# Gated SyncE loads and pairwise first score blocks in a windowed attention plus MLP kernel

## Chip, core, metric

One core of a Trainium2 chip. The metric is the device time of one execution in microseconds; five executions of the kernel before took 262.74 to 263.31 us, median 263.27.

## What is computed

Attention with a window and sinks over 4 batches, 8 heads, 768 positions, head size 64, and then a token mixer and a two-layer MLP on its output (width 512, hidden 2048). Cut to its core:

```python
# attention: q, k, v are (4, 8, 768, 64)
scores = matmul(q, k.T) / sqrt(64)
keep = (key < 4) | (0 <= query - key < 128)          # 4 sinks, window 128
a = softmax(where(keep, scores, -1e9))
x = (a @ v) as (4, 768, 512)
# mixer
a1 = alpha1 * x + beta1
u = x + lam * einsum('ts,bsd->btd', w_tok, a1)       # w_tok 768 x 768
a2 = alpha2 * u + beta2
out = u + lam * (relu(a2 @ w_ch1) @ w_ch2)           # 512 -> 2048 -> 512
```

Inputs and output are float32; the kernel's matmuls are float16.

## The kernel before

The kernel works in tiles of 128 positions: six row tiles per batch (r, j or ti), heads in four pairs (hp) and two groups of four heads (G).

The steps for a batch, with their lines:

- **Loads.** q and k of a head pair (`load_qk`, L481) come through SyncE's queue in float32, 384 KB each; six of batch 0 come through GpSimd's queue, which casts to float16 on the way (L486). v comes by row tiles (L503; batch 0 by halves, `load_v0`, L520), w_tok by row tiles of 384 KB (L531), w_ch2 in blocks of 512 KB (`load_w`, L540), w_ch1 in four quarters of its hidden columns through GpSimd's queue (`load_w1`, L544; 512 KB written each, twice that read), lam at L1156.
- **Transposes** of q and k on TensorE (L594, L597), copied out to `qkT` by ScalarE or VectorE (L349, L351); from batch 2 on by DMA (L613).
- **Scores.** Per key tile j, a block S (L702), in the first batch for one group of four heads. S has two buffers in PSUM. In the first batch most blocks first get a mask added by a matmul of the identity with a bias (L697); the others are multiplied by a mask on VectorE afterwards (L731). ScalarE takes the exponential (L722). The sinks have their own product and exponential (L639, L644).
- **pv** (L785, L792), and on VectorE the division by the sum (L817, L818) to x; then `xh` = x * lam * alpha1 on GpSimd (L827, L834), and the beta term on VectorE (L841).
- **tok** (L916): six matmuls per row tile with the transposed w_tok; VectorE adds it to x (L923), ScalarE or GpSimd cast to u.
- **uTp** (L957): transposes of u, and alpha2, beta2 applied on ScalarE and VectorE (L940, L942).
- **h** (L996): 16 blocks of 128 hidden columns for each half batch, relu on ScalarE or VectorE (L1002, L1004). A quarter of w_ch1 serves four blocks.
- **ch** (L1052, L1023): the second product. w_ch2 is first multiplied by lam on VectorE or GpSimd (L898), from the buffers that L540 filled.
- **Out**: VectorE adds (L1063, L1032) and SyncE stores (L1066, L1035).

Batches overlap: the attention of the next batch is worked in among the MLP of this one.

The order of the work isn't written out. Each step is added to a `Plan` as a task with a priority, an engine or a choice of them with a cost in ns, the tasks that it needs, and the buffers that it uses. `Plan.run` goes through modelled time and gives each engine the ready task that can start first, ties by priority; the result is the order in which each engine's instructions stand in the program, and the engines keep to it. The model has two DMA rings (`Rings`): SyncE's and GpSimd's, which share the engines by turns. When the model says that a transfer has landed, its task is seen as done 300 ns later (L203). Where the model sees TensorE idle before 36 us, filler matmuls on zeros are put in (`idle`, L342). `emit` shuffles the priorities with the seeds in `TURNS` (L406) before it runs the plan, so that each list of seeds gives another order. `W1_SINCE` (L407) lets no request for w_ch1 be planned before 20 us.

`scores_by_pair` (L739) scores a key tile of the first batch, first group, pair by pair: two blocks of half the size, each with its own exponential, and one mask product. It is used for j < `PAIRS`, and `PAIRS` is 0 (L404), so it isn't used. The choice is made here (L1121):

```python
            if G == 0 and j < PAIRS:
                scores_by_pair(base + 10 * j, j, BIAS[0][j])
            else:
                scores(base + 10 * j, 0, j, (G,), bias=BIAS[G][j])
```

The requests of SyncE's queue for the second batch stand at L1152 to L1162: q and k, lam, w_ch2, v. Nothing but buffers, the model's times and priorities orders them against w_ch1.

Of the kernel before, what the change touches and what calls it, by code (L numbers as in the profile page):

```python
# [10 lines left out]
FP16 = mybir.dt.float16  # L11
# [4 lines left out]
PE, ACT, DVE, POOL, SP = "pe", "act", "dve", "pool", "sp"  # L16
# [13 lines left out]


FW = 1.0


class Rings:
# [74 lines left out]
class Plan:  # L110
# [9 lines left out]
    def add(self, prio, engs, fn, after=(), uses=(), mode=None, lands=None, port=False,  # L120
            since=0.0):


        t = Task(len(self.tasks), prio, engs, fn, after, uses, mode, lands, port, since)
        for a in t.needs:
            a.then.append(t)
        self.tasks.append(t)
        return t

    def run(self, prio):  # L130
# [17 lines left out]
        rings = Rings()  # L148
# [3 lines left out]
        def end(t, seen):  # L152
            t.seen = seen
            for b in t.uses:
                b.left -= 1
                b.freed = max(b.freed, seen)
                if b.left == 0:
                    busy[b.kind][b.home] = False
                    homes[b.kind][b.home] = b.freed
            for o in t.then:  # L160
                ready[o.i] = max(ready[o.i], seen)
                waiting[o.i] -= 1
                if not waiting[o.i]:
                    bisect.insort(open_, (rank[o.i], o.i))
# [33 lines left out]
        while len(steps) < len(tasks):  # L198
            best = pick()
            if best is None or landing <= best[0]:  # L200
                assert landing < float("inf"), "no task can go on"
                t = rings.step(float("inf"))
                end(t, rings.now + 300.0)  # L203
                landing = rings.peek()
                continue
            start, r, _, i, e = best
            open_.pop(bisect.bisect_left(open_, (r, i)))
            t = tasks[i]
            for b in t.uses:
                if b.home is None:  # L210
                    b.home = min((h, n) for n, (h, x) in enumerate(zip(homes[b.kind], busy[b.kind]))
                                 if not x)[1]
                    busy[b.kind][b.home] = True
            idle = None
            n = int((start - max(free[PE], 400.0)) / (took if free[PE] > 4500.0 else 110.0))
            if e == PE and free[PE] < until and n > 0:
                spare = [(h, k) for k, (h, x) in enumerate(zip(homes["d"], busy["d"])) if not x]
                if spare and min(spare)[0] <= free[PE]:
                    idle = (min(spare)[1], n)
                    homes["d"][idle[0]] = start  # L220
                    mode = None
            cost = t.engs[e]
            if t.lands:
                cost += rings.room("sw" if e == POOL else "hw", t.lands, start) - start
            if e == PE:
                if start < 4500.0:
                    cost = cost * 2
                if t.mode != mode:
                    cost = cost + 95
                mode = t.mode  # L230
            free[e] = start + cost
            if e == POOL or (e == DVE and t.port):
                port = free[e]
            steps.append((t, e, start, free[e], idle))
            if t.lands:
                rings.step(start)
                rings.issue("sw" if e == POOL else "hw", t, free[e])
                landing = rings.peek()
            else:
                end(t, free[e] + SEEN[e])  # L240
# [34 lines left out]
def kernel(  # L275
# [123 lines left out]
    w1f = const.tile([P, NC, DFF], FP16, name="w1f")  # L399
    w2f = const.tile([P, NF, DM], FP16, name="w2f")  # L400

    ROWS = 7000.0

    PAIRS = 0  # L404

    TURNS = (39286, 39315, 39323, 39754, 40467, 41250, 41382, 139002, 39003, 39015, 139040, 139062, 139089, 139154, 39159, 139160, 39171, 39387, 139559, 139625, 139757, 139905, 39966, 140019, 140036, 140073)  # L406
    W1_SINCE = 20000.0  # L407

    V0 = (((0, 1), (2, 3), (4, 5)), ((0, 1, 2), (3, 4, 5)))
# [90 lines left out]
    def load_v(p, b, r, wait=None):  # L500
        bf = vn[b, r] = Buf("vnat", None, None, f"vnat{b}_{r}")
        done["vn", b, r] = add(
            p, {SP: 550}, lambda e: nc.sync.dma_start(  # L503
                bf.t, v[b, :, r * P : (r + 1) * P, :].rearrange("h p d -> p h d")),
            [wait], [bf], lands=(64, 19.0))
# [31 lines left out]
    def load_w(p, key, src):  # L537
        bf = wst[key] = Buf("wst", None, None, f"wst_{key}")
        done["wst", key] = add(
            p, {SP: 400}, lambda e: nc.sync.dma_start(bf.t, src), uses=[bf], lands=(16, 90))  # L540

    def load_w1(p, i):
        done["w1", i] = add(
            p, {POOL: 760}, lambda e: nc.gpsimd.dma_start(  # L544
                w1f[:, :, i * 512 : (i + 1) * 512],
                moe_w_ch1[:, i * 512 : (i + 1) * 512].rearrange("(c p) f -> p c f", p=P)),
            lands=(32, 96), since=W1_SINCE)

    def load_w2(p, i):
        for a in range(4 * i, 4 * i + 4, 2):  # L550
# [541 lines left out]
    load_w1(-770, 0)  # L1092
    for i in range(1, 4):
        load_w1(-769, i)

    def fold_rows():
        for name, key, o, p in (("a1", "la1", la1_b, -987), ("b1", "lb1b", lb1_b, -986)):
# [36 lines left out]
    for b in range(B):  # L1134
        w0 = STEP * b
        if b == 0:
            seq = [("tok", ti) for ti in range(3)] + [("uT", 0, 0), ("uT", 0, 1)]
            seq += [("tok", ti) for ti in range(3, NR)]
            m1 = []
            for qd in range(4):  # L1140
                for chk in range(2):
                    m1 += [("m1", chk, fi) for fi in range(4 * qd, 4 * qd + 4)]
            m1.insert(3, ("uT", 1, 0))
            m1.insert(5, ("uT", 1, 1))
        else:
            seq = [("tok", ti) for ti in range(NR)]
            m1 = [("m1", 0, fi) for fi in range(NF)]
            m1 += [("m1", 1, fi) for fi in range(NF)]
        seq += m1
        seq += [("m2", ti, part) for ti in range(NR) for part in range(4)]  # L1150
        ns = len(seq)
        if b == 0:  # L1152
            for i, (hp, t) in enumerate(QK_ORDER):
                load_qk(t0 + 100 + i, 1, hp, t)
            done["lam"] = add(
                t0 + 150, {SP: 500}, lambda e: nc.sync.dma_start(  # L1156
                    lam_b, moe_lam.unsqueeze(0).to_broadcast([P, DM])), lands=(8, 90))
            for i in range(4):
                load_w2(t0 + 200 + i, i)
                cast_w2(w0 + 22 + 4 * i, i)  # L1160
            for r in range(NR):
                load_v(t0 + 300 + r, 1, r)  # L1162
        for i, (what, *args) in enumerate(seq):

            p = w0 + i - (LEAD if b and what == "tok" and args[0] < 3 else 0)
            {"tok": tok, "uT": uTp, "m1": mlp1, "m2": mlp2}[what](p, b, *args)
            if b and what == "tok":
                uTx(p + 0.3, b, *args)
        if b + 1 < B:
            nb = b + 1  # L1170
            if nb >= XB:
                for i, (hp, t) in enumerate(QK_ORDER):
                    load_qk(w0 + i, nb, hp, t, done["qkT", b, 3, 1])
                for r in range(NR):
                    load_v(w0 + 10 + r, nb, r, done["qkT", b, 3, 1])
            lo, hi = (1, ns - 14) if b else (LO, ns - 12)
            steps = [("T", i) for i in range(8)] + [("sk",)]
            for j in range(NR):
                steps += [("S", j)]
                steps += [("pv", j - 1, 0), ("pv", j - 1, 1)] if j else [("vs",)]  # L1180
            steps += [("pv", NR - 1, 0), ("pv", NR - 1, 1)]
            for r in range(NR):
                cast_v(w0 + lo + (hi - lo) * (r + 4) / len(steps), nb, r)
            for i, (what, *args) in enumerate(steps):
                p = w0 + lo + (hi - lo) * i / len(steps) + 0.5
                if what == "T":
                    hp, t = QK_ORDER[args[0]]
                    trans(p if nb < XB else w0 - 15 + i, nb, hp, t, {POOL: 829, ACT: 831}, {DVE: 955, ACT: 800},
                          wait=done["tok", b, 2])
                elif what == "sk":  # L1190
                    sinks(p, nb)
                elif what == "vs":
                    fill_vs(p, nb)
                elif what == "S":
                    j = args[0]
                    scores(p, nb, j, (0, 1) if j < NR - 1 else (None,))
                else:
                    pv(p, nb, *args)
# [37 lines left out]
```

The softmax here doesn't subtract the row's maximum and nothing guards it: scores larger than these inputs give would overflow.

## Time and profile before

| what | value |
|---|---|
| median of 5 executions | 263.27 us |
| the profiled execution's own time | 263.27 us |
| its span in the profile | 261.6 us |
| TensorE (PE) busy | 253.5 us, 97% |
| VectorE (DVE) busy | 155.1 us, 59% |
| ScalarE (ACT) busy | 134.2 us, 51% |
| GpSimd (POOL) busy | 81.9 us, 31% |
| granted TensorE clock, mean | 0.998 |
| w_ch1 requests, time to landing | 10.8, 15.6, 15.8, 19.0 us |
| w_tok requests, time to landing | 5.0 to 14.7 us |

The profile is of one execution. PE's busy time counts fillers too, so 97% isn't the share of useful work. A row of the timeline has the start, the length, the engine, the line, what is written and read, and how many such instructions follow each other; in brackets stands the idle time of the engine before it and what ended it. A row of the stages has for each engine the busy time and the number of instructions, then the granted clock (1.00 is full), the mean busy share of the DMA engines (over 1 where packets overlap) and GB/s. DMA sizes are counted as written: a casting load from float32 to float16 reads twice that.

### The profile page before, as it was taken

The page shows a single profiled execution, that of the slowest core. Times are in us where ns is not written, and L with a number is a line of the kernel's source. Part 1 is how long each engine was busy: PE and PEld are TensorE (multiplying, and loading weights), DVE is VectorE, ACT ScalarE, POOL GpSimd, SP SyncE. Part 2 cuts the span into 40 slices and gives each one's busy share as a digit, 9 for nine tenths or more (in the row PEclk, how much of TensorE's full clock was granted, in tenths as well). Part 3 has the DMA queues.
Part 4 walks back from the last instruction along what each step waited for, and adds up shares of the span by engine and source line. Part 5 has one row for each costly group of instructions (what it writes and reads, how often), then busy time and mean ns, then how long its engine had stood idle before and what let it go on. Part 6 is the DMA issues. An engine that isn't in the chain of part 4 may idle for free.

```text
span 261.6 us, 4960 instructions
## 1 busy us (share of the span) xinstructions
PE 253.5 (97%) x1954; PEld 139.8 (53%) x1954; DVE 155.1 (59%) x315; ACT 134.2 (51%) x219; POOL 81.9 (31%) x100
## 2 busy tenths in 40 slices
PE   7899989999999999999999999999999999999994
PEld 6554656465555544565545445556555445565453
DVE  4697994778999937755668534559965444000222
ACT  1788657579782224767741126788411137773000
POOL 8539952355612511244427203004222000000000
PEclk9999999999999999999999999999999999999999
DMA  7999999969976998999827669300012233000222
GB/s 175 197 214 374 302 290 276 316 146 309 187 126 169 247 189 182 190 218 220 159 57 166 166 127 235 77 0 3 0 41 83 70 91 83 0 0 3 81 80 80
DMA packets 85791, 38.76 MB, mean 148 GB/s; under 512 B 73460, under 2 KB 79868, under 8 KB 85768
## 3 DMA queue, kind: packets, MB, share of 16 engines
q1 hardware_dynamic: 81984, 35.14, 57.0%
q0 software_dynamic: 3744, 3.28, 7.6%
q8 instruction: 15, 0.25, 0.4%
q14 instruction: 8, 0.07, 0.1%
q10 hardware_dynamic: 40, 0.03, 0.0%
HBM read 29.91 MB, written 6.29 MB: 138 GB/s over the span
## 4 chain that ended last, share of the span: by engine, by line
PE 82%; DMA 11%; POOL 3%; DVE 2%; issue 0%; POOLq 0%
PE ch L1052 31%; PE h L996 28%; PE tok L916 9%; DMA w1f<-in_moe_w_ch_dram 7%; PE pv L792 4%; PE S L702 4%; DMA n<-in_k_dram 4%; PE S L697 1%; PE ch L1023 1%; POOL n L486 1%; POOL xh L827 1%; PE pv L785 1%; DVE x L841 1%; DVE E L731 1%; PE sk L639 1%; DVE x L818 0%
## 5 line engine op out<-in xcount | busy, mean ns | idle before, releaser
L996 PE MATMUL h<-uT,w1f 128*128 128x384 f16 x512 | 89.2, 326 | 0.8 <-DMA w1f<-in_moe_w_ch_dram 0.4
L1052 PE MATMUL ch<-w2f,hT 128*128 128x512 f16 x368 | 86.5, 379 | 0.1
L996 PEld LDWEIGHTS <-w1f 128*128 128x128 f16 x512 | 48.1, 98 | 34.2 <-issue 3.3
L1002 ACT ACTIVATE hT<-h 128x384 f16<-128x384 f32 x103 | 50.2, 491 | 24.6 <-PE h L996 24.0
L1052 PEld LDWEIGHTS <-hT 128*128 128x128 f16 x368 | 34.4, 98 | 38.1 <-issue 1.0
L722 ACT ACTIVATE E<-S 128x1024 f16<-128x1024 f32 (+1 forms) x42 | 40.6, 1003 | 12.3 <-PE S L702 10.6
L834 POOL TENSOR_TENSOR xh<-x,la_b 128x512 f16<-128x512 f32 x18 | 25.7, 1431 | 51.1 <-DVE x L818 29.8
L1063 DVE TENSOR_TENSOR x<-x,ch 128x512 f32<-128x512 f32 x23 | 15.8, 686 | 35.0 <-PE ch L1052 35.0
L916 PE MATMUL tok<-xh,wtokT 128*128 128x512 f16 x144 | 33.7, 379 | 0.0
L349 ACT CAST u<-x 128x512 f16<-128x512 f32 x17 | 10.5, 618 | 42.4 <-DVE x L923 42.4
L923 DVE TENSOR_TENSOR x<-x,tok 128x512 f32<-128x512 f32 x24 | 16.3, 687 | 19.9 <-PE tok L916 19.8
L841 DVE SCALAR_TENSOR_TENSOR x<-lb_b,rsum,x 128x512 f32<-128x512 f32 x24 | 23.0, 970 | 5.2 <-POOL xh L834 4.9
L1004 DVE TENSOR_SCALAR hT<-h 128x384 f16<-128x384 f32 x25 | 13.9, 555 | 17.7 <-PE h L996 17.2
L916 PEld LDWEIGHTS <-wtokT 128*128 128x128 f16 x144 | 13.9, 98 | 16.3
L818 DVE TENSOR_TENSOR x<-pv,rec 128x256 f32<-128x256 f32 x48 | 20.4, 425 | 1.7
L351 POOL CAST vfs<-vnat 128x512 f16<-128x512 f32 x18 | 13.4, 749 | 19.9 <-DMA vnat<-in_v_dram 15.7
L792 PEld LDWEIGHTS <-E 128*128 128x128 f16 x328 | 15.1, 97 | 6.3 <-issue 0.6
L731 DVE TENSOR_TENSOR E<-E,maskn 128x1024 f16<-128x1024 f16 x25 | 18.0, 740 | 0.0
L792 PE MATMUL pv<-vfs,E 128*128 128x65 f16 x328 | 17.8, 194 | 0.0
L351 POOL CAST u<-x 128x512 f16<-128x512 f32 x7 | 5.2, 742 | 37.6 <-DVE x L923 37.6
L351 POOL CAST n<-nat 128x768 f16<-128x768 f32 x12 | 10.1, 851 | 15.8 <-DMA nat<-in_q_dram 7.7
L349 ACT CAST n<-nat 128x768 f16<-128x768 f32 x12 | 9.9, 832 | 8.1 <-DMA nat<-in_k_dram 7.5
(99 smaller groups left out, 206.3 us busy)
## 6 DMA issues: line engine op xcount, KB each, us to landing
out_dram<-x SPq DMA_DIRECT2D x23, 256.0 KB, 2.4
nat<-in_q_dram SPq DMA_DIRECT2D x13, 384.0 KB, 5.7
nat<-in_k_dram SPq DMA_DIRECT2D x13, 384.0 KB, 6.7
vnat<-in_v_dram SPq DMA_DIRECT2D x18, 256.0 KB, 4.5
wst_w<-in_moe_w_ch_dram SPq DMA_DIRECT2D x8, 512.0 KB, 11.8
wtn<-in_moe_w_tok_dram SPq DMA_DIRECT2D x6, 384.0 KB, 5.3
w1f<-in_moe_w_ch_dram POOLq DMA_DIRECT2D x4, 512.0 KB, 15.7
v<-in_v_dram SPq DMA_DIRECT2D x12, 128.0 KB, 6.7
```

Source lines behind the costliest of these rows:

```text
L349: nc.scalar.copy(o, i)
L351: engine[e].tensor_copy(o, i)
L722: nc.scalar.activation(eT.t, pS.t[:, :, 0 : n * w].rearrange("p e (i w) -> p e i w", i=n), AF.Exp, scale=scale)
L731: nc.vector.tensor_mul(ev, ev, m.to_broadcast(list(ev.shape)))
L792: nc.tensor.matmul(po.t[:, hl, :], eT.t[:, e_, off + i, c : c + P], vf[j][:, h, :], start=(r < 2 and n == 0), stop=(n == len(parts) - 1 an ...
L818: nc.vector.tensor_mul(bx.t[:, 4 * G : 4 * G + 4, :], po.t[:, :, 0:D], rec.t.to_broadcast([P, 4, D]))
L834: engine[e].tensor_mul(bh.t, bx.t.rearrange("p h d -> p (h d)"), la1_b)
L841: engine[e].scalar_tensor_tensor(out=xf, in0=lb1_b, scalar=rsum[:, r : r + 1], in1=xf, op0=ALU.mult, op1=ALU.add)
L916: nc.tensor.matmul(pt.t, wtokT[:, si, ti * P : (ti + 1) * P], hs[si].t, start=(si == 0), stop=(si == NR - 1))
L996: nc.tensor.matmul(ph.t, w1f[:, c, fi * P : (fi + 1) * P], bu.t[:, c, chk * NTOK : (chk + 1) * NTOK], start=(c == 0), stop=(c == NC - 1))
L1002: nc.scalar.activation(bh.t[:, fi, :], ph.t, AF.Relu)
L1052: nc.tensor.matmul(pc.t, bh.t[:, fi, nt * P : (nt + 1) * P], w2f[:, fi, :], start=(fi == 0), stop=(fi == NF - 1))
```

## The change

Four things are edited.

1. **Gates.** A new task `gate(i)` issues on SyncE's queue a DMA of eight elements from quarter i of w_ch1 in SBUF to a small tile. Since it reads what the load of the quarter writes, SyncE waits there until the quarter has landed; all that stands behind it in SyncE's order is asked for later. In the plan, w_ch2's loads need quarter 1, q and k of the second batch need quarter 2, and v of the second batch needs quarter 3 (these needs act on the planned order; the gate's own wait is what holds the queue).
2. **SWDONE.** The model sees a transfer of GpSimd's queue as done 1800 ns after it has landed in the model, in place of 300.
3. **PAIRS = 3**: key tiles 0, 1 and 2 of the first batch, first group, are scored by pairs.
4. **TURNS**: another list of 16 seeds, where there were 26.

```diff
+SWDONE = 1800.0
...
-                end(t, rings.now + 300.0)
+                end(t, rings.now + (SWDONE if POOL in t.engs else 300.0))
...
+    gates = const.tile([1, 32], FP16, name="gates")
+
+    GATES = (1, 2, 3)
...
-    PAIRS = 0
+    PAIRS = 3
...
-    TURNS = (39286, 39315, 39323, 39754, 40467, 41250, 41382, 139002, 39003, 39015, 139040, 139062, 139089, 139154, 39159, 139160, 39171, 39387, 139559, 139625, 139757, 139905, 39966, 140019, 140036, 140073)
+    TURNS = (13523, 134113, 50022, 128275, 136711, 187603, 125671, 100730, 14946, 163131, 178432, 158827, 183776, 137680, 153375, 26742)
...
     def load_w(p, key, src):
         bf = wst[key] = Buf("wst", None, None, f"wst_{key}")
         done["wst", key] = add(
-            p, {SP: 400}, lambda e: nc.sync.dma_start(bf.t, src), uses=[bf], lands=(16, 90))
+            p, {SP: 400}, lambda e: nc.sync.dma_start(bf.t, src), [done.get(("w1", GATES[0]))], uses=[bf], lands=(16, 90))
...
+    def gate(i):
+
+        add(-3000, {SP: 420}, lambda e: nc.sync.dma_start(
+            gates[0:1, 8 * i : 8 * i + 8], w1f[0:1, 0, i * 512 : i * 512 + 8]), [done["w1", i]],
+            lands=(1, 20))
...
+    for i in sorted(set(GATES)):
+        if i < 0:
+            continue
+        gate(i)
...
-                load_qk(t0 + 100 + i, 1, hp, t)
+                load_qk(t0 + 100 + i, 1, hp, t, done.get(("w1", GATES[1])))
...
-                load_v(t0 + 300 + r, 1, r)
+                load_v(t0 + 300 + r, 1, r, done.get(("w1", GATES[2])))
```

What this makes of the order, read from the two built programs:

- SyncE before: half tiles of v, q and k of the first pair, the other v, four tiles of w_tok, a w_ch2 block, six q and k loads of the second batch, two tiles of w_tok, two q and k, lam, three w_ch2 blocks, then v and w_ch2 by turns. After: one tile of w_tok, q and k of the first pair, all v, the other five tiles of w_tok, lam, gate 1, four w_ch2 blocks, gate 2, six q and k, gate 3, two q and k, four w_ch2 blocks, six v.
- GpSimd before: identity, six casting loads, masks; after: the small selection masks, two casting loads, identity, three casting loads, masks, the last casting load. w_ch1's quarters are asked before as 1, 2, 3, 0, the first two after five half-tile products xh of the first group; after as 0, 1, 2, 3, each behind two more such products.
- TensorE before has done four w_tok transposes, four of tok's six row tiles and four q and k transposes of the second batch when h begins; after, all six w_tok transposes, all six tiles of tok and none of the second batch. Those stand among the h blocks, after the 13th. Fillers: 88 before, 106 after.
- VectorE after begins with the cast of a w_tok tile and the copy of its transpose, in front of the cast of q.

## The prediction

> **What bounds the kernel now.** I read the busy time by stage first, then the chain of waits, then TensorE's timeline. The stages (TensorE is the first busy figure of a row):
>
> ```profile
> 0.00:30.00 30.00, 27.05 (x364) 17.26 (x365) 21.86 (x66) 20.43 (x28) 21.25 (x40) 1.00 1.02 251
> 30.00:38.76 8.76, 7.78 (x65) 4.59 (x64) 8.42 (x13) 4.59 (x7) 5.91 (x8) 1.00 1.14 284
> 38.76:58.00 19.24, 18.53 (x137) 11.30 (x138) 12.48 (x22) 12.83 (x26) 7.84 (x9) 1.00 1.01 256
> 58.00:258.00 200.00, 199.93 (x1392) 106.68 (x1389) 111.69 (x216) 96.31 (x159) 46.94 (x45) 1.00 0.55 117
> ```
>
> From 58 to 258 us TensorE is idle for 0.07 of 200 us: the change can only lose there. What can be won lies before 58: idle of 2.95, 0.98 and 0.71 us, and fillers (matmuls on zeros while TensorE waits):
>
> ```profile
> L342 PE MATMUL idle<-warm x88: 219/220/315, 1.1 to 27.4; 128*128 128x128 f16 x88
> ```
>
> In the timeline the first 45 take 4.21 us (91 ns apart), the next 14 take 0.95 (56 ns apart), so all cost about 45 x 0.091 + 43 x 0.056 = 6.5 us. The chain of waits leaves the start of the kernel through w_ch1:
>
> ```profile
> 27.27 0.43 DVE x L818
> 27.77 1.41 POOL xh L827 x2
> 29.18 0.75 POOL w1f L544
> 29.96 0.57 POOL xh L827
> 30.64 0.67 POOL xh L827
> 31.32 19.02 DMA w1f<-in_moe_w_ch_dram
> 50.38 2.12 PE h L996 x12
> ```
>
> That looks like 19 us of transfer on the path, but it is not: TensorE had other work in it. Its timeline shows what it really waited for:
>
> ```profile
> 37.45 0.84 PE L957 MATMUL uTp<-iden,u 128*128 128x128 f16 x12 [0.64 <-POOL u L351]
> 39.40 1.46 PE L996 MATMUL h<-uT,w1f 128*128 128x384 f16 x7 [0.31 <-DVE uT L942]
> 50.38 2.12 PE L996 MATMUL h<-uT,w1f 128*128 128x384 f16 x12 [0.40 <-DMA w1f<-in_moe_w_ch_dram]
> ```
>
> So w_ch1's lateness costs 0.40 us, and the order of work was bent around it.
>
> **The gates.** Rates first, from single transfers in the tile view. A w_tok tile asked at 17.0 lands 5.0 later (22.0); the w2 block asked at 19.0 lands at 26.2, with three more w_tok tiles between them: 1.70 MB in 4.2 us, 405 GB/s. With w_ch1 beside it the same queue is slower: a k load asked at 20.05 lands at 28.5, the last one at 45.7, eight loads of 393 KB in 17.2 us, 183 GB/s. The quarters land at 34.5, 40.1, 44.9, 50.3: 1.05 MB read each 5.3 us, 199 GB/s. Both queues share about 400.
>
> In the changed program SyncE asks for w_tok and lam, then gate, four w2 blocks, gate, six q/k, gate, two q/k, w2, v. The first quarter is asked behind two half-row products, by the walk below at 20.9; the four are asked by 28.3. I put quarter 0 at 29, quarter 1 at 33, quarter 2 at 36.5, quarter 3 at 41. No h matmul waits for them: 0.40 saved. Behind gate 1 (33) w2's first two blocks come at 38 and 41, since they share with quarters 2 and 3; then alone at 1.3 us each to 44, and q/k 1.0 us each: 45 to 52. Who waits: VectorE has the first w2 product (L909) in its order ahead of the second uT chunk; it gets there at 41. GpSimd's q/k casts (0.83 each) stand behind a w2 product too, and TensorE wants the first transposes at 49.6 and the last at 56. Slack 2 to 3 us, so I cost the gates at nothing; without it, each us late is a us on TensorE. The gate instructions cost SyncE 3 x 0.4 (its issue rows), with nothing else behind them.
>
> A rule speaks against this: the Trainium skill, "DMA: Bandwidth & Descriptors", Rules for kernel authors, says to issue a DMA early and wait late, so that its fixed cost (about 2.0 us in "Anatomy of one DMA") is hidden. By it three gates would start w2, q/k and v up to 3 x 2.0 = 6 us later and eat the slack: 3 us slower. The row is against it: a w2 block asked at 32.5 landed 17.1 us later. Asking early bought a place behind other bytes, and w_ch1 keeps the engines full through the waits (DMA share 1.14). I take the row.
>
> **The start, walked in the new order.** The seeds and constants reorder everything before 41 us, so I go through the instruction order with the durations of before.
>
> Head: SyncE's first transfer is now a w_tok tile, 393 KB / 405 = 1.0 us ahead of q and k. VectorE casts it (0.94 + 0.08, to 5.1) and copies its transpose (0.55) before q's cast, which ends at 6.9 (before: 5.98). GpSimd does sel first, which waits for a VectorE memset at 1.64 + 0.11, so its casting loads start at 2.65 (before 1.50) and the masks end at 8.3; VectorE's bias pair (0.45) waits for them, in front of k's cast: 9.45 (before 7.96). ScalarE then copies four transposes (0.80 each) to 11.85.
>
> Pair scoring brings the first exponential forward, since it needs two of these copies and not four, but they are queued on ScalarE anyway: 11.85, before 12.01. It costs six ACTIVATEs for three:
>
> ```profile
> L722 ACT ACTIVATE E<-S 128x1024 f16<-128x1024 f32 x10 | 10.1, 1023 | 1.6 <-PE S L702 1.5
> L722 ACT ACTIVATE E<-S 128x512 f16<-128x512 f32 x2 | 1.2, 594 | 0.8 <-PE S L702 0.8
> ```
>
> 6 x 0.594 - 3 x 1.023 = +0.5 us on ScalarE, whose order now runs to the last exponential: six of 0.55 (start to start), seven of 0.95, two of 0.55, sinks 1.05, two v casts 1.68, a transpose copy 0.75, ks 0.3, a w_tok cast 1.07 = 15.9. Waits: 0.45 for sinks and scores, and 0.45 at ks, where VectorE's last transpose copy stands behind the cast of v rows 3 (landing 15.9 before, 16.9 now). 11.85 + 15.9 + 0.9 = 28.65, say 28.4 to 28.7 (before 28.17). Fillers: 106, 35 of them first, 0.9 us more; they fill waits counted here already.
>
> From there: two w_tok casts on ScalarE (1.05 each), two wtokT copies (0.8 each) to 32.1. TensorE starts tok at 29.85 (before 29.52), but with w_tok transposed further. tok runs as 4 + 4 + 2 + 6 + 2 + 6 matmuls (0.215 each) with one transpose (0.34): 35.4. Then it waits 0.55: four banks are full, and VectorE has five L841 (0.97 back to back, from 30.3) in front of the first L923. Two more tok (1.29 each): 38.6. uTp and its affine take 1.95, as from 37.45 to 39.40 before: h runs from 40.5.
>
> Before it ran from 39.40, with less done: two tok (2.59) and two w_tok transposes (0.68) fewer, four q/k transposes (1.34) more, net 1.93. Equal would be 41.33. Gain 0.83.
>
> **Sum.** 0.83 + 0.40 - allowance 0.5. The allowance: a hand walk misses small waits (the trace has 2.4 us of ScalarE waiting at L722 in six pieces, my walk 0.9), and w_tok's last tile, at 183 GB/s beside w_ch1, would land at 30.4 against its cast at 29.5. Gain 0.73. The profiled execution took 263.27, 1.67 around its span of 261.6; that equals the median 263.27. 263.27 - 0.73 = **262.5**.
>
> Unknown costs. Mode changes of TensorE before the first h: 40 for 30; at about 0.13 each (an S block's 4 matmuls take 0.32 against 4 x 0.055) +1.3 if none were hidden, -0 if all; they fall where TensorE waits for ScalarE, so 0. The gate's read of landed w_ch1: 0 to 2 us of SyncE per gate, hidden while slack holds. The steps after 58: 0 to +1, nearer 0, as before has none.
>
> **Rivals.** (1) The front is later: w_tok's tiles share with w_ch1, ScalarE's two casts wait to 28.3 and 30.4, and v's landing holds VectorE 1 us longer. For: all that is tight there. Against: w_tok's rows are long. 1 + 0.7 lost in place of 0.73 won: **264.2**. (2) The gates bind: if quarter 1 lands after 36 (as at 5.3 us a quarter from 25.5), w2's second block comes after 43.5 and VectorE's queue holds the uT chunk; q/k then reach the casts after 49. Price about 2 us: **264.8**. Against: quarter 0 is asked some 2.8 us earlier than before's 23.7. (3) What the front wins is lost in small waits; the transfer was hidden anyway: **263.2**. (4) Pair scoring does its work: ScalarE runs from 11.1, as it would if q's cast weren't held by the bias, and no allowance is needed: 262.5 - 0.75 - 0.5 = **261.2**.
>
> **Numbers.** Forecast 0.38, (4) 0.14, (3) 0.18, (1) 0.18, (2) 0.12. A measurement tells 0.2% (0.53 us) from no change, so the forecast lies close to the edge of faster; a quarter of it counts as same. Faster 0.14 + 0.30 = 0.44, same 0.25, slower 0.31. Range 260.8 to 264.9.
>
> **What would show it.** First exponential near 11.9 and the last near 28.5; h running from 40.5; no wait of L1007 for w1f, quarter 1 landed by 34, quarter 3 by 42; no wait of VectorE or GpSimd at L909 for w2. TensorE idle below 0.2 us after 58. I am wrong if h starts after 41.5, if VectorE waits at a w2 product with uT behind it, or if a stall shows after 58.

## The result and the profile after

The changed kernel takes 262.36 us (median of 27 executions, 261.49 to 263.90), the kernel before beside it 263.34 us (48 executions). The ratio is 0.9963, with a 95% interval of 0.9949 to 0.9976: a gain of 0.98 us where 0.73 was forecast. The profiled execution took 261.65 us, 1.62 less than that of before, with a span of 259.9 us. The difference between the two gains is a first hint: the 27 executions aren't all alike, and seven of them took more than 263 us. They spread from 261.5 to 263.9 us without a clear gap; the line at 263 us, used below, is drawn by eye.

The busy time by stage, in the same columns as before:

```profile
0.00:30.00 30.00, 28.37 (x394) 19.31 (x395) 22.78 (x70) 22.20 (x35) 19.26 (x37) 1.00 1.07 231
30.00:38.76 8.76, 8.76 (x56) 4.51 (x55) 8.17 (x13) 3.66 (x7) 1.06 (x2) 1.00 1.20 245
38.76:58.00 19.24, 18.13 (x155) 11.79 (x152) 15.01 (x24) 13.80 (x27) 8.37 (x9) 1.00 1.04 369
```

From 30 to 38.76 us TensorE has no idle time left (0.98 before). From 38.76 to 58 it has more (1.11 against 0.71), which looks like a loss and isn't one. TensorE's timeline shows where it lies:

```profile
38.07 0.83 PE L968 MATMUL uTp<-iden,u 128*128 128x128 f16 x12
39.38 0.32 PE L1007 MATMUL h<-uT,w1f 128*128 128x384 f16 x1 [0.47 <-ACT uT L951]
39.89 0.71 PE L1007 MATMUL h<-uT,w1f 128*128 128x384 f16 x2 [0.19 <-DVE uT L953]
40.98 2.27 PE L1007 MATMUL h<-uT,w1f 128*128 128x384 f16 x13 [0.38 <-ACT uT L951]
```

The wait between the transposes of u and the first h product is 1.04 us in three pieces, and it now falls into this stage. After 41 us no wait is listed, and w_ch1 is in none of the brackets. Three h products at 0.162 each were done before 40.98, so h runs in effect from 40.49; equal to before would have been 41.33. The last long run of h, 128 products, in the chain of waits of the kernel before and of the changed one:

```profile
216.70 20.80 PE h L996 x128
214.82 20.80 PE h L1007 x128
```

It begins 1.88 us earlier. Of these, 0.84 are won by the first h, and 0.40 are the wait for w_ch1 that before had on the way from there; for the other 0.64 us the timelines list no wait.

### The profile page after: what moved, and what is told of

The parts are those of the page before. It is cut to its first block, busy times and chain, and to the rows that moved or that the text cites. A ratio compares the mean times of both kernels' runs of the same rounds, so it can differ in the third digit from the quotient of the medians.

```text
span 259.9 us, 4992 instructions
## 1 busy us (share of the span) xinstructions
PE 253.6 (98%) x1974; PEld 141.1 (54%) x1974; DVE 155.9 (60%) x321; ACT 132.7 (51%) x219; POOL 79.4 (31%) x97
## 2 busy tenths in 40 slices
DMA packets 85839, 38.76 MB, mean 149 GB/s; under 512 B 73508, under 2 KB 79916, under 8 KB 85816
## 4 chain that ended last, share of the span: by engine, by line
PE 94%; POOL 2%; DVE 1%; issue 1%; ACT 1%; POOLq 0%; ACTq 0%
PE h L1007 32%; PE ch L1063 31%; PE tok L927 12%; PE pv L803 5%; PE S L713 4%; PE S L708 1%; PE ch L1034 1%; POOL n L491 1%; PE tp L608 1%; PE pv L796 1%; PE tp L605 1%; PE idle L344 1%; PE wT L887 1%; PE sk L650 1%; ACT uT L951 1%
## 5 line engine op out<-in xcount | busy, mean ns | idle before, releaser
L1007 PEld LDWEIGHTS <-w1f 128*128 128x128 f16 x512 | 48.5, 98 | 33.8 <-issue 3.2
L1013 ACT ACTIVATE hT<-h 128x384 f16<-128x384 f32 x100 | 48.8, 490 | 28.4 <-PE h L1007 27.7
L733 ACT ACTIVATE E<-S 128x1024 f16<-128x1024 f32 (+1 forms) x39 | 37.5, 1001 | 7.3 <-PE S L713 4.7
L845 POOL TENSOR_TENSOR xh<-x,la_b 128x512 f16<-128x512 f32 x18 | 24.3, 1353 | 54.4 <-DVE x L829 54.2
L351 ACT CAST u<-x 128x512 f16<-128x512 f32 x18 | 11.1, 618 | 43.0 <-DVE x L934 42.9
L852 DVE SCALAR_TENSOR_TENSOR x<-lb_b,rsum,x 128x512 f32<-128x512 f32 x24 | 19.3, 821 | 2.8 <-POOL xh L845 2.6
L742 DVE TENSOR_TENSOR E<-E,maskn 128x1024 f16<-128x1024 f16 x24 | 19.4, 831 | 1.8 <-ACT E L733 1.7
L1015 DVE TENSOR_SCALAR hT<-h 128x384 f16<-128x384 f32 x28 | 15.4, 555 | 8.0 <-PE h L1007 7.5
L803 PEld LDWEIGHTS <-E 128*128 128x128 f16 x328 | 14.4, 97 | 6.5 <-issue 2.4
L353 POOL CAST n<-nat 128x768 f16<-128x768 f32 x14 | 12.2, 878 | 14.4 <-DMA nat<-in_k_dram 12.5
L353 POOL CAST u<-x 128x512 f16<-128x512 f32 x6 | 3.7, 620 | 37.3 <-DVE x L934 15.5
L953 DVE TENSOR_SCALAR uT<-uT,ab 128x384 f16<-128x384 f16 x18 | 6.4, 409 | 12.3 <-DMA uT<-u 12.3
```

Source lines behind the costliest of these rows:

```text
L353: engine[e].tensor_copy(o, i)
L733: nc.scalar.activation(eT.t, pS.t[:, :, 0 : n * w].rearrange("p e (i w) -> p e i w", i=n), AF.Exp, scale=scale)
L742: nc.vector.tensor_mul(ev, ev, m.to_broadcast(list(ev.shape)))
L803: nc.tensor.matmul(po.t[:, hl, :], eT.t[:, e_, off + i, c : c + P], vf[j][:, h, :], start=(r < 2 and n == 0), stop=(n == len(parts) - 1 an ...
L845: engine[e].tensor_mul(bh.t, bx.t.rearrange("p h d -> p (h d)"), la1_b)
L852: engine[e].scalar_tensor_tensor(out=xf, in0=lb1_b, scalar=rsum[:, r : r + 1], in1=xf, op0=ALU.mult, op1=ALU.add)
```

## Experiments

Times are medians, ratios are to the kernel before, run beside each on the same chip (263.12 to 263.34 us). The last column counts the executions above 263 us.

| kernel | gates | pairs | us | ratio, 95% interval | above 263 |
|---|---|---|---|---|---|
| changed | yes | 3 | 262.36 | 0.9963, 0.9949 to 0.9976 | 7 of 27 |
| changed, again | yes | 3 | 262.23 | 0.9975, 0.9957 to 0.9994 | 5 of 14 |
| no gates | no | 3 | 261.55 | 0.9944, 0.9927 to 0.9960 | 0 of 6 |
| no gates, again | no | 3 | 261.66 | 0.9943, 0.9926 to 0.9959 | 0 of 6 |
| no pairs | yes | 0 | 262.99 | 0.9996, 0.9984 to 1.0009 | 10 of 22 |
| order alone | no | 0 | 262.10 | 0.9955, 0.9940 to 0.9971 | 0 of 9 |
| first pair only | yes | 1 | 263.23 | 0.9994, 0.9980 to 1.0009 | 9 of 14 |
| first pair only, no gates | no | 1 | 262.09 | 0.9958, 0.9941 to 0.9974 | 0 of 6 |
| gate 1 reads quarter 2 | yes | 3 | 261.73 | 0.9950, 0.9933 to 0.9967 | 0 of 6 |
| all gates read quarter 3 | yes | 3 | 264.13 | 1.0045, 1.0026 to 1.0064 | 17 of 19 |
| v behind one more gate | yes | 3 | 262.27 | 0.9963, 0.9950 to 0.9976 | 0 of 11 |

All of these keep the changed kernel's order on every engine, except for what is taken out, joined or added. That order was itself planned with pairs and gates, and no run separates what SWDONE and what the seeds did to it.

### The gates taken out

```diff
-        add(-3000, {SP: 420}, lambda e: nc.sync.dma_start(
-            gates[0:1, 8 * i : 8 * i + 8], w1f[0:1, 0, i * 512 : i * 512 + 8]), [done["w1", i]],
-            lands=(1, 20))
+        add(-3000, {SP: 420}, lambda e: None, [done["w1", i]], lands=(1, 20))
```

> The changed kernel's order on every engine, without the three gate instructions: SyncE asks for w_ch2, q and k, and v as soon as lam is asked for. Theory (the order carries the gain, the gates little): w_ch1 shares the engines again, a quarter every 5.3 us from about 32, so quarter 1 lands near 37.5 and quarter 3 near 48; the first h block wants quarter 1 at 39.4 and quarters 2 and 3 are wanted after 52: 0 to +0.5 us, 262.4 to 262.9. Rival (the gates carry it): quarter 1 lands after 39.4 by a microsecond or more, TensorE waits for it at its first h block, 263.3 or more.

261.55 us, below what the theory and the rival said: without gates the kernel is 0.8 us faster (0.6 us in the second set of runs). The transfers did what the gates are there to prevent: from single transfers, the quarters of w_ch1 landed at 33.8, 39.1, 44.3 and 49.0 us, with gates at 30.6, 33.6, 36.1 and 38.8. TensorE has the same three waits for uT before its first 16 h products; a weight load stood 0.6 us for w_ch1, and no product waited on it. So w_ch1's earlier landing is hidden, and what removed the 0.40 us of before is the order of the work, not the gates.

### How late a gate may open

```diff
+        r = max(i, 2)
...
-            gates[0:1, 8 * i : 8 * i + 8], w1f[0:1, 0, i * 512 : i * 512 + 8]), [done["w1", i]],
+            gates[0:1, 8 * i : 8 * i + 8], w1f[0:1, 0, r * 512 : r * 512 + 8]), [done["w1", i]],
```

Gate 1 (and what is behind it) waits for quarter 2; in the second kernel, with 3 in place of 2, all gates wait for quarter 3 (the lines shown are the first kernel's).

> The changed kernel, the first gate reading quarter 2 of w_ch1 in place of quarter 1, so that SyncE's queue opens at 36.1 and not 33.6, 2.5 us later. Theory (slack of 2 to 3 us behind the gates): TensorE waits at most 0.3 us more, 262.3 to 262.7. Rival (the gates already bind): each us late is a us on TensorE, 264.4 or more.

> The changed kernel, all gates reading quarter 3, landed at 38.8: SyncE's queue opens 5.2 us later. Theory (slack of 2 to 3 us): TensorE waits 2 to 3 us, for q and k of the second batch or for VectorE held at a w_ch2 product, 264.4 to 265.4. Rival (no slack): 267 or more; rival (the order has far more slack than 3 us, the transfers are hidden anyway): under 263.

The first gate opened at 36.0 and 39.6 us in place of 33.6. The 2.4 us cost nothing: 261.73 us is even below the changed kernel, but with six executions the intervals overlap. The 6.0 us cost 1.8 (264.13). In the list of what TensorE waited for after 38 us, the second kernel has

```profile
PE uTp L969 <- DVE hT L1016: 1.6, 1, 1.6
PE h L1008 <- ACT uT L952: 1.5, 3, 0.6
```

(engine, line and releaser, then us in total, times, longest). VectorE stood 3.2 us at a w_ch2 product whose block hadn't landed, with hT behind it. The slack that the prediction put at 2 to 3 us is more than 2.4 us and, as 6.0 us later cost 1.8, about 4.

### The pairs taken out, and order alone

Key tiles 0 to 2 are scored as whole blocks, at the place in the order of their second pair (`hp == 1`); the second kernel also has no gates. The matmuls of the whole block aren't shown.

```diff
             def mm(e, hp=hp, pS=pS):
+                if hp == 0:
+                    return
...
             def ex(e, hp=hp, pS=pS):
-                nc.scalar.activation(eT.t[:, :, hp, :], pS.t[:, :, 0:w], AF.Exp, scale=scale)
+                if hp == 0:
+                    return
+                nc.scalar.activation(
+                    eT.t, pS.t[:, :, 0 : 2 * w].rearrange("p e (i w) -> p e i w", i=2),
+                    AF.Exp, scale=scale)
```

> The changed kernel's order, but key tiles 0 to 2 of the first group scored as one block each, at the place of the second pair, with one ACTIVATE of 1024 columns for two of 512. Theory (pairs bring nothing, as the first exponential waits in ScalarE's queue): the last exponential of the start stays within 0.3 us of 28.0, time 262.2 to 262.7. Rival (pair scoring does its work): ScalarE stands idle from 11.7 to the second pairs and does three exponentials of 0.95 where 0.55 stood, the last exponential 0.6 us later, time 262.9 to 263.1.

> The changed kernel's order with neither gates nor pairs. Theory (pairs are worth 0.9 us, gates nothing): 262.7 to 263.2, as the kernel before, first exponential at 13.1. Rival (the order by itself wins, and gates and whole blocks only disturb one another): 262.3 or less. Other rival (without gates the whole blocks' later end meets a later w_ch1): above 263.6.

262.99 us with gates and 262.10 without. The first is what the rival said: pairs do bring something. The second missed what my theory of that moment said ("as the kernel before"): the order by itself beats the kernel before by 1.0 us. Read as a square with the kernels above, the pairs are worth 0.55 us without gates (262.10 to 261.55) and 0.63 with them (262.99 to 262.36). With gates the intervals of 262.99 and 262.36 don't touch (those of 262.99 and the second run, 262.23, do); without gates they overlap, so the 0.55 alone isn't clear of noise. ScalarE's timeline shows what the pairs do. The changed kernel:

```profile
10.99 0.80 ACT L351 COPY qkT<-tp 128x768 f16<-128x768 f16 x1 [0.33 <-PE tp L605]
11.69 1.09 ACT L771 ACTIVATE E<-S 128x512 f16<-128x512 f32 x2
12.71 0.59 ACT L655 ACTIVATE es<-sk 64x512 f16<-64x512 f32 x1
13.24 0.60 ACT L771 ACTIVATE E<-S 128x512 f16<-128x512 f32 x1
14.11 1.02 ACT L733 ACTIVATE E<-S 128x1024 f16<-128x1024 f32 x1 [0.27 <-PE S L713]
```

Order alone:

```profile
11.00 0.80 ACT L351 COPY qkT<-tp 128x768 f16<-128x768 f16 x1 [0.19 <-PE tp L603]
12.66 0.59 ACT L653 ACTIVATE es<-sk 64x512 f16<-64x512 f32 x1 [0.86 <-PE sk L648]
13.52 1.02 ACT L731 ACTIVATE E<-S 128x1024 f16<-128x1024 f32 x1 [0.27 <-PE S L711]
```

The last of the four copies ends at the same time. A whole block can only be multiplied after it, so ScalarE stands 0.86 + 0.27 us. The first pair's products need only the first two copies: the exponentials at 11.69 (two) and 13.24 are the first halves of key tiles 0, 1 and 2, and they fill that time; their second halves come after 15. The last exponential ends at 28.00 in the changed kernel, at 28.69 with order alone and 28.87 without pairs. tok begins at 29.77 to 30.16 in the four profiles of the changed kernel with and without gates, with whole blocks at 30.29 without gates and 30.46 with them.

### One pair only

As above, with `if j == 0` around the pair's form, so that key tile 0 alone is scored by pairs; the second kernel without gates.

> Only key tile 0 of the first group is scored by pairs; key tiles 1 and 2 are whole blocks at the place of their second pair, all else as in the changed kernel. Theory (the pairs are worth some 0.9 us because the first exponential runs before the second pair's copies, 11.7 in place of 13.1): all of it is at key tile 0, so no slower than the changed kernel, 262.0 to 262.5, first exponential at 11.7, last one ended by 28.0; two ACTIVATEs fewer could even save 0.3. Rival (each half block keeps ScalarE and TensorE going further on): 262.7 to 263.1, last exponential ended after 28.4.

> Pairs at key tile 0 only, and no gates. Theory (what this kernel lost with gates was GpSimd's casts of v beside VectorE's products, which the profile of its execution at 263.9 shows, and not the pairs): 261.5 to 261.9, none above 263. Rival (two whole blocks after one pair are slow by themselves): 262.8 to 263.4, as with gates.

263.23 and 262.09 us. Both theories missed the time. One pair alone brings nothing: 262.09 us is order alone's 262.10, and 263.23 isn't below 262.99. ScalarE's timeline without gates shows why:

```profile
11.88 0.60 ACT L770 ACTIVATE E<-S 128x512 f16<-128x512 f32 x1
12.88 0.59 ACT L653 ACTIVATE es<-sk 64x512 f16<-64x512 f32 x1 [0.40 <-PE sk L648]
13.75 1.02 ACT L731 ACTIVATE E<-S 128x1024 f16<-128x1024 f32 x1 [0.27 <-PE S L711]
14.67 0.59 ACT L770 ACTIVATE E<-S 128x512 f16<-128x512 f32 x1
15.79 0.80 ACT L351 COPY qkT<-tp 128x768 f16<-128x768 f16 x1 [0.54 <-PE tp L603]
```

The first exponential is early, but ScalarE then stands 0.40 + 0.27 + 0.54 us, as long as with whole blocks, because the first halves of key tiles 1 and 2 aren't there to follow. The last exponential ends at 29.02 without gates and 28.86 with them, and tok begins at 30.61 and 30.45: late, as the rival of the first kernel said.

That kernel also shows the cost of the gates. Its profiled execution took 263.92 us, so the trace is of one of the long ones, which the changed kernel's isn't. The stage after 58 us holds 1.29 us of idle TensorE there. The timeline of VectorE, GpSimd and that wait:

```profile
58.53 0.62 POOL L353 CAST vfs<-vnat 128x512 f16<-128x512 f32 x1 [4.42 <-DMA vnat<-in_v_dram]
...
58.57 3.80 DVE L934 TENSOR_TENSOR w2f<-wst_w,lam_b 128x512 f16<-128x512 f32 x3
...
59.43 0.74 POOL L353 CAST vfs<-vnat 128x512 f16<-128x512 f32 x1 [0.28 <-DMA vnat<-in_v_dram]
...
60.13 1.70 POOL L934 TENSOR_TENSOR w2f<-wst_w,lam_b 128x512 f16<-128x512 f32 x1
...
62.30 1.09 DVE L742 TENSOR_TENSOR E<-E,mask 128x1024 f16<-128x1024 f16 x1
63.31 0.54 DVE L1040 TENSOR_SCALAR hT<-h 128x384 f16<-128x384 f32 x1
...
63.91 0.49 PE L1032 MATMUL h<-uT,w1f 128*128 128x384 f16 x2 [1.29 <-DVE hT L1040]
```

The same instructions in the changed kernel's profile, which is of a short execution:

```profile
57.52 1.89 DVE L909 TENSOR_TENSOR w2f<-wst_w,lam_b 128x512 f16<-128x512 f32 x3
...
59.06 1.83 POOL L353 CAST vfs<-vnat 128x512 f16<-128x512 f32 x2 [5.01 <-DMA vnat<-in_v_dram]
...
59.32 1.10 DVE L742 TENSOR_TENSOR E<-E,mask 128x1024 f16<-128x1024 f16 x1
```

Three of VectorE's w_ch2 products take 1.89 us when all three have begun before GpSimd's casts of v (the third at 58.72), and 3.80 when a cast begins first. VectorE then stands before hT, and TensorE before h. A profile of another kernel with gates, with the bias behind the cast (below), lies between:

```profile
57.57 2.30 DVE L917 TENSOR_TENSOR w2f<-wst_w,lam_b 128x512 f16<-128x512 f32 x3
...
58.68 0.65 POOL L358 CAST vfs<-vnat 128x512 f16<-128x512 f32 x1 [5.00 <-DMA vnat<-in_v_dram]
```

Here a cast begins 0.09 us ahead of the third product only, which then takes 1.10 us; TensorE stands 0.2 us for an hT later.

There is a second meeting, and the gates make it. In the eight profiles with gates (without the one on quarter 3) GpSimd's own w_ch2 product waits 1.2 to 2.9 us for its block and begins at 41.2 to 42.9, during VectorE's first two or just behind them; in the four without gates it begins at 39.3 to 40.1, ahead of them. In the trace of 263.92 us one of VectorE's products, at 41.83, takes 1.76 us beside it; by 58.57 VectorE is 0.3 us later than in the same kernel without gates (58.28).

The Trainium skill, "SBUF — State Buffer", section "SBUF: two separate sides", says that a VectorE operation with two SBUF inputs and a GpSimd operation that reads SBUF exclude each other for the length of an instruction, and the one that begins first holds the port. The rows agree: by the single instructions, the third product begins at 60.63, GpSimd's product (60.13, 1.70 us) ends at 61.83, and VectorE is done 0.55 us after that, where a whole product alone takes 0.68.

### v held back

If the meeting with the casts of v is what makes long executions, v only has to come later. One more gate, on the w_ch2 product that VectorE ends at 57.0 (the first two loads of v are also placed behind that product in the program, by lines not shown):

```diff
+        def ld(e):
+            if (b, r) == (1, 0):
+                nc.sync.dma_start(gates[0:1, 0:8], w2f[0:1, 8, 0:8])
+            nc.sync.dma_start(bf.t, v[b, :, r * P : (r + 1) * P, :].rearrange("h p d -> p h d"))
```

> The changed kernel with one more gate: SyncE's v loads of the second batch stand behind a read of the w2 product that VectorE writes at 56.3 to 57.0, so GpSimd's casts of v begin at 60.5 to 61 and not at 59.1. Theory (with the gates v comes early enough that GpSimd's casts run beside three of VectorE's w2 products, which then take twice as long, in some executions and not in others): the products at 57.5 take 1.9 us, the upper part of the changed kernel's times (8 of 27 above 263.1) is gone, median 261.5 to 261.9. Rival (the upper times come from elsewhere, or v is simply needed): 262.3 to 263.5, as many above 263.

> The changed kernel once more, on the chip of these runs: 262.0 to 262.7, with a quarter to a third of its executions above 263 and the others near 262.

> The changed kernel without its three gates, once more. Theory (the gates cost up to 0.8 us through the casts of v): 261.4 to 261.8, none above 263. Rival (its earlier six runs were a lucky draw): 262.0 to 262.7, as the changed kernel beside it.

(Seven, not eight, of the 27 are above 263.1.) The changed kernel again had 5 of 14 executions above 263 us, v held back 0 of 11 and no gates 0 of 6. In the profile with v held back the casts begin at 61.27, and the three products take 1.88 us. The theory's half on the spread held; its level was missed (262.27, not 261.5 to 261.9). The list of TensorE's waits after 58 us says why:

```profile
PE h L1016 <- DVE vs L681: 0.5, 1, 0.5
```

Held back by this much, v is late for its first use: 0.5 us in the profiled execution, where the changed kernel's executions above 263 us, about a third, are some 1.4 us longer than its others (263.4 and 262.0 in the middle).

Without gates, v's casts begin at 60.4 (first run and order alone), 60.0 (first pair only) and 59.07 (again); with gates, in the seven profiles that neither hold v back nor wait for quarter 3, at 58.5 to 60.6. The ranges overlap, so the profiles don't show that the gates bring v earlier. At 59.07 the cast overlaps the third product by 0.5 us, but the product began first, and the cast lasted longer.

Over all kernels of the table without gates, 0 of 27 executions are above 263 us; with the gates of the change, 31 of 77. That the gates make the long executions, in this order, is shown. That v's casts are the decisive piece is likely and not shown: for it stand v held back (0 of 11, where the changed kernel has 12 of 41) and two traces. The second meeting, at GpSimd's w_ch2 product, wasn't tested apart, and gate 1 on quarter 2 has 0 of 6 with all its gates. How much of the 0.4 us between the short executions with gates (262.0) and those without (261.6) comes from smaller meetings of this kind stays open too; in the second set of runs it is only 0.1 us (261.76 and 261.66).

### The head

GpSimd's masks hold VectorE 1.28 us at the bias, in front of k's cast. In one kernel the bias pair is made behind that cast; in another the memset of the selection masks is also moved forward, so that GpSimd begins earlier:

```diff
+        steps.remove(late[0])
+        at = [s[0] for s in steps].index(self.behind)
+        steps.insert(at + 1, late[0])
...
+    sel = const.tile([P, P], FP16, name="sel")
+    nc.vector.memset(sel, 0.0)
```

> VectorE makes the two bias tiles, which wait for GpSimd's masks, behind the cast of k instead of ahead of it; all else as in the changed kernel. Theory (the wait of 1.28 us holds the head, but ScalarE meets VectorE's last transpose copy at 18.2 and the landing of v anyway): first exponential 0.3 to 0.9 earlier, the last one at most 0.3 earlier, 261.9 to 262.4. Rival (the head is the path; what ScalarE wins at its first exponential it keeps): 261.3 to 261.6.

> As the one before, and the memset of the selection masks is done third on VectorE, so that GpSimd's casting loads and masks start some 0.8 us earlier. Theory (the rest of the head is slack): within 0.2 us of the one before, 261.8 to 262.4. Rival (v's landing and the masks set the end of the exponentials): 0.4 to 0.8 us below it, 261.0 to 261.5.

262.57 us (ratio 0.9987, 0.9965 to 1.0009) and 262.75 (0.9981, 0.9968 to 0.9994), both above what their theories said: no gain over the changed kernel, and both have gates and executions above 263 us (5 of 14 and 10 of 22). In the first the exponentials begin at 11.30 in place of 11.69, but ScalarE then waits 0.20 us for the sinks' score product and 0.16 for a transpose, and tok begins at 30.01 in place of 29.96. So in that profile the 0.39 us of head are slack. The second says nothing on that: in its profile k landed later (VectorE waits 0.91 us for it), and the exponentials begin at 11.95.

## Why the prediction was right, and which steps of it weren't

The time (262.36 for 262.5) and the main cause, an order with more of the first batch's mixer done before h begins, were right. That the time is so close is luck: two terms were wrong and cancel. By its steps:

- **h runs from 40.5**: 40.49. tok begins at 29.96 (29.85 said), the first exponential at 11.69 (11.85), the last one ends at 28.00 (28.4 to 28.7).
- **A wait of 0.55 us for a PSUM bank in tok**: it wasn't there. The term had five L841 at 0.97 us back to back; the five (now L852) took 3.62 us, 0.72 each. tok ended at 38.07, not 38.6, and this half microsecond went into uT's three waits (1.04 us), so that h began where it was put: luck here too.
- **0.40 us of w_ch1 saved**: saved, but not by the gates; without them it is saved too.
- **The allowance of 0.5 us**: not needed in the profiled execution (1.62 us gained, more than 0.83 + 0.40). In the median it was, for a cause that the step didn't name.
- **The gates cost nothing**: the slack was found, if too small, and 2.4 us later is free. But the step asked only who waits for a transfer, and not what an engine meets when its work begins at another time: the term should have been +0.6 to +0.8 us. The remark in the list of signs, that TensorE is idle for less than 0.2 us after 58, holds in the changed kernel's profile and fails in the one long execution that a trace shows (1.29 us, first pair only).
- **Pairs bring nothing**: wrong by 0.55 to 0.63 us. The step compared first exponentials (11.85 and 12.01) and left out what follows the last copy: a whole block's product, 1.13 us of standing ScalarE, which the first halves of three key tiles fill. Less the +0.5 us of more ACTIVATEs that is near the gain measured. Rival (4) had the mechanism by name, but as a start at 11.1 with the head freed of the bias; ScalarE began at 11.69, and a freer head brought nothing.
- **Landings**: quarter 1 was put at 33 and landed at 33.6, quarter 3 at 41 and landed at 38.8, 2.5 to 3.0 us a quarter where 5.3 was the row of before. GpSimd did wait at L909 for w_ch2 (1.9 us, against "no wait"), and so its product began during VectorE's; what that costs isn't separated.

The two wrong terms, gates and pairs, are of nearly the same size and of opposite sign; the sum was good to 0.14 us because they cancel. The rule on early issue, which I set aside, pointed the right way: three gates fewer is 0.6 to 0.8 us faster. Its reason, as I priced it, 6 us of fixed cost and 3 us of time, didn't show: opening the first gate 2.4 us later still cost nothing.

The kernel to keep is the changed one without its gates: 261.55 and 261.66 us in two sets of runs, 0.9944 and 0.9943 of the kernel before. Beside the changed kernel itself the intervals overlap a little, so its lead over that one rests on both sets together and on the missing long executions.

## What to carry to other kernels

When a transfer's landing moves, either way, ask which engine begins work when it lands, and what else runs at that moment. When the times of one kernel spread over 2 us, count them before believing a profile, since the trace may be of the other kind. Splitting the first blocks of a pipeline pays where the engine behind them would stand until the last input of a whole block is there, if enough first halves are split off to fill that time: here three did, and one brought nothing.

## What was not expected of the hardware

- A w_ch2 product of VectorE (128x512, two inputs in SBUF) takes 0.68 us alone, and 1.1 to 1.8 us in these traces when a GpSimd cast or product began first. A shift of tenths of a microsecond decides which it is.
- With SyncE's queue held back, a quarter of w_ch1 landed 10.0 to 11.6 us after its request, and without the gates 13.3 to 22.0. Those up to 10 us decided nothing here.
- A gate's read of eight elements took 0.66 to 0.81 us of SyncE's queue each, where loads take 0.4.
